# Batch 0's queries in two loads, and the first weights, sums and transposes of a one-core attention and feed-forward kernel in another order

## The chip, the cores and the metric

The kernel runs on one core of one Trainium2 chip. The metric is the device time of one execution in microseconds (us); for a version the median of its runs counts. All times below come from the runs, or from one profiled execution and its trace.

## The reference

Eight batches of linear attention with cosine-weighted features, then a feed-forward layer whose two last products have no nonlinearity between them.

```python
# q, k, v: (8, 8, 576, 64) FP32; w1, w2: (512, 1024); w3: (1024, 1024); w_out: (1024, 512)
theta = np.pi / 2.0 * pos / S                                     # S = 576
phi(x) = concat([relu(x) * cos(theta), relu(x) * sin(theta)], -1) # 64 -> 128 features
kv  = einsum('bhsf,bhsd->bhfd', phi(k), v);   z = phi(k).sum(2)
num = einsum('bhsf,bhfd->bhsd', phi(q), kv)
den = einsum('bhsf,bhf->bhs', phi(q), z)[..., None] + 1e-06
x = (num / den).transpose(0, 2, 1, 3).reshape(8 * 576, 512)       # 4608 tokens
out = ((x @ w1) * (x @ w2)) @ w3 @ w_out
```

## The kernel before, in words

Matmul operands are BF16, sums FP32. The work is written as a list (PLAN) that is walked line by line; each word issues the instructions of one small step on whichever engines it needs, and every engine executes its own instructions in the order in which they were issued. So the list is the schedule, and nothing reorders it.

A batch has 576 positions, held as five chunks: 0 to 3 of 128 rows, 4 of 64. `k b c` and `q b c` make the features of a chunk: the cosine half on DVE (L504), the sine half on ACT (L508) or, for some heads, on DVE (L511). `qt` transposes a chunk of query features on PE (L576) into the PSUM tile pst and copies it to qpT (L580, on ACT or DVE). `kv b` (for batch 0 `kv0`, `ks0`) sums keys times values over the chunks on PE and `kvs0` or the end of `kv` copies the result (kvs). `n b c` is the numerator and denominator of a chunk (L594), `d b c` its division on DVE (L605 to L607, tile xblk), `xt b c` the transpose of the divided rows on PE (L636) with a copy into xT (L637). From batch 1 on most transposes are DMA transposes on SP (`qd`, `xd`).

The feed-forward part goes over nine tiles t of 512 tokens. Each `f t` is one step of it: products of xT with w1 and w2 (L683), the copy of the first (ACT) and its product with the second (DVE, tile abT), then abT times w34b (L766 for tile 0). w34b is w3 times w_out, made once: `t3` transposes a 128-row block of w3 on DVE (L473), `w jp` multiplies it with w_out on PE (L483), and ACT copies the result (L486). Tile 0's products stand ahead of that work, tile 0's output behind it, and batch 1's attention between.

Loads are issued by POOL (GpSimd) from FP32 in memory to BF16, in this order: keys and values of batch 0 (L384), eight blocks of w1 and w2 (`w12`, L980, 256 columns each), then w_out (`wo`, L421) and w3 (`w3`, L415) in quarters by partitions, the last chunk of batch 0's queries (`q04`), then batch 1. A load of POOL goes out only when the eighth load before it has landed. Batch 0's queries, chunks 0 to 3, come on SP's queue at the very start, FP32 to FP32, into q0f. Later loads stand behind a gate: a one-element copy by POOL from a tile that must be written first (`lg` behind asb, `lt` behind a transpose, `lx` behind a division). `idle n` issues n matmuls on zeros that nobody reads (L466).

Of the kernel before, what the change touches and what calls it, by code (L numbers as in the profile page):

```python
# [10 lines left out]
FP32 = mybir.dt.float32  # L11
BF16 = mybir.dt.bfloat16
# [4 lines left out]
P = 128  # L17
H, S, D = 8, 576, 64
# [5 lines left out]
WHOLE = (0, 7)  # L24
MORE = 8
PLAN = """\
q 0 1; idle 1; idle 1; q 0 0 4; idle 1; idle 1; qt 0 1 V; k 0 4; k 0 1 0; qs 0 3; k 0 0 0; k 0 2; idle 1; k 0 3; qt 0 0 A; ks0 4; idle 3; qc 0 3; ks0 1; kv0 4 0; q 0 2; kv0 1 0; ks0 0; kv0 2 0; kv0 4 1; ks0 3; kv0 0 0; ks0 2; kv0 0 1; kv0 3 0; kvs0 0 A; kv0 1 1; kv0 2 1; kv0 3 1; kvs0 1 V; qt 0 2 A; n0 0; n0 1; qt 0 3 N; w12 0 0 2; w12 1 0 2; w12 0 2 2; n 0 1; idle 2; w12 1 2 2; w12 0 4 2; d 0 0; w12 1 4 2; w12 0 6 2; w12 1 6 2; wo 0 0 4; d 0 1; qy 0 3 0 A; xt 0 0 A; wo 1 0 4; wo 2 0 4; wo 3 0 4; w3 0 0 2; w3 1 0 2; w3 2 0 2; w3 3 0 2; w3 0 2 2; w3 1 2 2; w3 2 2 2; w3 3 2 2; wo 0 4 4; wo 1 4 4; ns 0 2; idle 2; qy 0 3 1 V; d 0 2; wo 2 4 4; wo 3 4 4; w3 0 4 2; w3 1 4 2; w3 2 4 2; w3 3 4 2; q04; w3 0 6 2; w3 1 6 2; open; w3 2 6 2; w3 3 6 2; l 1 q 0; l 1 q 1; l 1 k 0
f 0; xt 0 1 A; n 0 3; l 1 k 1
f 0; d 0 3; l 1 v 0
f 0; xt 0 2 A  # L30
f 0
f 0; xt 0 3 V; l 1 v 1
f 0
f 0
f 0
f 0
f 0; clear 1
f 0
f 0
f 0; t3 0  # L40
f 0; lg 2 q 0; t3 1; l 2 k 0; l 2 k 1; l 2 q 1; l 2 v 0
f 0
f 0; t3 2 0 4; t3 3 0 4; t3 2 4 4; t3 3 4 4
w 0 0 4
# [17 lines left out]
f 0  # L62
f 0; qt 1 0 A; v 1 2 V; v 1 3 V
f 0
f 0; kv 1; qt 1 1 A
f 0; n 1 4; d 1 4; k 2 4; k 2 2 2
f 0
# [1 line left out]
f 0; n 1 0; d 1 0; xt 1 4 A; q 2 0 0; q 2 1; lt 3 v 0; xt 0 4 A  # L69
f 0  # L70
f 0; v 2 0 G
f 0
f 0; xt 1 0 V; n 1 1
f 0
f 0
f 1
f 1; lg 3 q 1; d 1 1; qd 2 0; n 1 2; v 2 3 A; k 2 3; d 1 2; qt 1 3 V
# [31 lines left out]
f 2; xd 3 0; n 3 1  # L109
f 2; d 3 1  # L110
f 2; xd 3 1
f 2; q 4 0; q 4 4; n 3 4
f 2; d 3 4; xd 3 4; lg 5 v 0; l 5 v 1
f 2
f 2; q 4 3; v 4 4 V
f 2; q 4 1 0
f 2; k 4 1; k 4 0; qd 4 0; n 3 2
f 2
f 2
f 2; q 4 2  # L120
f 2; lg 5 k 0; l 5 k 1
f 2
f 2; qd 4 3; d 3 2; n 3 3
f 3; k 4 4; k 4 2
# [198 lines left out]
def kernel(  # L323
# [11 lines left out]
    nc = tc.nc  # L335
    B = q.shape[0]
    DM, DFF = moe_w1.shape
# [4 lines left out]
    const = ctx.enter_context(tc.tile_pool(name="const", bufs=1))  # L342
# [19 lines left out]
    osbs += [q0f[:, ts(i, H // 2)].rearrange("p h c d -> p (h c d)").rearrange("p (i m) -> p i m", m=DM) for i in range(2)]  # L362

    def osb_of(i):

# [13 lines left out]
    raw = {}  # L379

    def load_rows(eng, t, rows, half):

        j, span = (5, slice(0, 320)) if half == 0 else (4, slice(320, S))
        eng.dma_start(out=t[ts(half, 64), :, 0:j, :].rearrange("p h j d -> p h (j d)"),  # L384
                      in_=rows[:, span, :].rearrange("h (p j) d -> p h (j d)", j=j))

    def load(b, name, part=None):
        src = {"k": k, "v": v, "q": q}[name]
        if part != 1:
            raw[b, name] = kbufs[b % 2] if name == "k" else ld.tile([P, H, NCH, D], BF16, name=name + "s", bufs=NRQ if name == "q" else NRV)  # L390
        t = raw[b, name]
        if b == 7:
            if part != 1:
                nc.gpsimd.dma_start(out=t[:, :, 0:4, :].rearrange("p h j d -> p h (j d)"),
                                    in_=src[b, :, 0:512, :].rearrange("h (p j) d -> p h (j d)", j=4))
# [29 lines left out]
    def gate(behind):  # L425

        nc.gpsimd.tensor_copy(out=seen[0:behind.shape[0]], in_=behind)  # L427

    def load_q04():
# [33 lines left out]
    def idle_mms(n):  # L463

        for _ in range(n):
            nc.tensor.matmul(unread[:, :], lhsT=zeros[:, 0:128], rhs=zeros[:], start=True, stop=True)  # L466

    idle_mms(16)
    def w3_tr(jp, l0=0, n=8):

        if l0 == 0:
            w3Ts[jp] = sm.tile([P, 8, 128], BF16, name="w3T", bufs=NT3)
        nc.vector.transpose(out=w3Ts[jp][:, l0:l0 + n, :].rearrange("p l (c i) -> p l c i", c=4),  # L473
                            in_=w3b[:, jp, :].rearrange("p (c l j) -> p l c j", c=4, l=8)[:, l0:l0 + n])
# [19 lines left out]
    def att_of(b):  # L494
        if b not in att:
            att[b] = {"kp": kp_bufs[b % NKP], "qp": qp_bufs[b % NQP], "va": va_bufs[b % NVA],
                      "qpT": qpT_bufs[b % 2], "x": {}, "n": {}}
        return att[b]

    def features(dst, rows, c, at, n=H, cos=True, sin=True):  # L500

        R = ROWS[c]
        if cos:
            nc.vector.tensor_scalar(out=dst[:R, c, :, 0:D], in0=rows[:R], scalar1=0.0,  # L504
                                    scalar2=cosv[:R, at:at + 1], op0=ALU.max, op1=ALU.mult)
        if sin:
            if n > 0:
                nc.scalar.activation(out=dst[:R, c, 0:n, D:F], in_=rows[:R, 0:n], func=ACTF.Relu,  # L508
                                     scale=sinv[:R, at:at + 1], bias=0.0)
            if n < H:  # L510
                nc.vector.tensor_scalar(out=dst[:R, c, n:H, D:F], in0=rows[:R, n:H], scalar1=0.0,  # L511
                                        scalar2=sinv[:R, at:at + 1], op0=ALU.max, op1=ALU.mult)

    def prep_k(b, c, n=H, **kw):
        features(att_of(b)["kp"], raw[b, "k"][:, :, c, :], c, NCH + c if b == 7 else c, n, **kw)

    def prep_q(b, c, n=H, **kw):
        rows = raw[b, "q"][:, :, c, :] if b > 0 else q0f[:, :, c, :] if c < 4 else q04[:]
        features(att_of(b)["qp"], rows, c, NCH + c if b in WHOLE else c, n, **kw)

    def prep_v(b, c, copy=None):
# [440 lines left out]
    N = None  # L962
    V, A, G = nc.vector.tensor_copy, nc.scalar.copy, nc.gpsimd.tensor_copy
# [43 lines left out]
    def store_behind_transposes():  # L1007
# [4 lines left out]
    ffn = [ffn_groups(t) for t in range(NT)]  # L1012
    do = {
        "f": lambda t: next(ffn[t]), "w": w34_mm, "w3": load_w3, "wo": load_wout, "w12": w12,
        "l": load, "lg": gated, "lt": behind_transposes, "lx": behind_division, "q04": load_q04, "gx": behind_first_x,
        "k": prep_k, "q": prep_q, "v": prep_v,
        "qc": lambda b, c: prep_q(b, c, sin=False), "qs": lambda b, c, n=H: prep_q(b, c, n, cos=False),
        "kc": lambda b, c: prep_k(b, c, sin=False), "ks": lambda b, c: prep_k(b, c, cos=False),
        "qt": q_tr, "qy": q_copy, "ns": lambda b, c: num(b, c, pfirst), "qh": q_tr_halves, "qd": q_dma, "kv": kv, "kv0": lambda c, *half: kv_first(c, False, *half), "ks0": lambda c: kv_first(c, True), "kvs0": kvs_first,
# [40 lines left out]
```

## Time and profile before

| | us |
|---|---|
| median of 3 runs | 243.5 (242.95 to 244.08) |
| the profiled execution | 243.63 |
| its span | 241.9 |
| PE busy | 234.9 |
| DVE busy | 194.6 |
| ACT busy | 112.9 |
| POOL busy | 81.3 |

The span runs from the first to the last instruction of the profile; the execution's time has 1.73 us around it. Busy times are per engine and overlap. Rows of the timeline give start, length, engine, line, instruction, the tiles it writes and reads, and, in brackets, how long the engine had idled and what ended that. The chain of waits follows the last instruction back to what released it, step by step.

### The profile page before, as it was taken

Reading aid. Unit: us, or ns where it says so; the run is one execution under the profiler, and the core shown is the slowest. Engines: PE = TensorE matmul, PEld = TensorE weight load, DVE = VectorE, ACT = ScalarE, POOL = GpSimd, SP = SyncE. Lnnn points to the kernel's source line nnn. Section 1 sums busy time; section 2 is a strip of 40 time slices with the busy share of each in tenths; the row PEclk is TensorE's granted clock in tenths of the full one; section 3 lists DMA queues with packets and bytes.
Section 4 is the critical chain, followed back from the end, with each engine's and each line's share of the span. In section 5 each row is a group of like instructions: output and inputs, shape, how many; then the busy total and the mean of one; then the engine's idle time right before and its main releaser. Section 6 shows DMA issues by size and latency. Waiting matters only on the chain.

```text
span 241.9 us, 5817 instructions
## 1 busy us (share of the span) xinstructions
PE 234.9 (97%) x2236; PEld 163.6 (68%) x2236; DVE 194.6 (80%) x470; ACT 112.9 (47%) x200; POOL 81.3 (34%) x151
## 2 busy tenths in 40 slices
PE   8899999999999999999999999999999999999993
PEld 2579544566964595688679848875995698484462
DVE  6874585978988947999899998999999788776461
ACT  2754314587755832826465435637164302312321
POOL 8763888541804222700430312021020040272020
PEclk9999999999999999999999999999999999999999
DMA  6999999999999999999999959888456938599934
GB/s 196 192 197 199 164 195 186 198 199 194 178 166 147 128 152 198 181 173 180 132 179 177 114 96 184 149 131 90 76 191 129 130 70 160 115 308 311 259 97 173
DMA packets 84939, 40.48 MB, mean 167 GB/s; under 512 B 48048, under 2 KB 82096, under 8 KB 84912
## 3 DMA queue, kind: packets, MB, share of 16 engines
q0 software_dynamic: 37616, 23.60, 66.2%
q1 hardware_dynamic: 47296, 16.52, 40.4%
q8 instruction: 17, 0.28, 0.4%
q14 instruction: 10, 0.08, 0.1%
HBM read 38.80 MB, written 9.44 MB: 199 GB/s over the span
## 4 chain that ended last, share of the span: by engine, by line
PE 77%; DMA 14%; POOL 5%; DVE 1%; issue 1%; ACT 1%; ACTq 0%; POOLq 0%
PE ffnps L683 46%; PE ffnps L874 13%; DMA kf<-in_k_dram 7%; PE ffnps L766 6%; DMA w2b<-in_moe_w_dram 5%; PE pnum L594 4%; PE pnum L558 4%; DMA early<-in_moe_w_out_dram 2%; POOL early L415 2%; PE ffnmore L874 1%; PE ffnps L807 1%; PE ffnps L783 1%; POOL w2b L980 1%; POOL kf L384 1%; POOL w1b L980 1%
## 5 line engine op out<-in xcount | busy, mean ns | idle before, releaser
L683 PE MATMUL ffnps<-xT,w1b 128*128 128x256 bf16 (+2 forms) x448 | 76.2, 303 | 0.2 <-PE unread L466 0.2
L683 PE MATMUL ffnps<-xT,w2b 128*128 128x256 bf16 (+2 forms) x448 | 76.2, 303 | 0.0
L683 PEld LDWEIGHTS <-w1b 128*128 128x128 bf16 x448 | 41.1, 98 | 19.4 <-issue 1.0
L683 PEld LDWEIGHTS <-w2b 128*128 128x128 bf16 x448 | 40.8, 98 | 19.7 <-issue 0.2
L743 ACT CAST asb<-ffnps 128x512 bf16<-128x512 f32 x40 | 23.4, 585 | 43.0 <-PE ffnps L683 38.4
L749 DVE TENSOR_TENSOR abT<-asb,ffnps 128x512 bf16<-128x512 bf16 x40 | 27.2, 682 | 13.8 <-PE ffnps L683 13.5
L726 ACT CAST asb<-ffnps 128x512 bf16<-128x512 f32 x24 | 14.0, 584 | 34.2 <-PE ffnps L683 27.0
L607 DVE TENSOR_TENSOR xblk<-pnum,den 128x512 bf16<-128x512 f32 (+1 forms) x38 | 26.3, 691 | 1.5
L427 POOL COPY seen<-asb 128x1 bf16<-128x1 bf16 x17 | 3.4, 201 | 60.2 <-ACT asb L726 49.7
L508 ACT ACTIVATE kp<-kf,sinv 128x512 bf16<-128x512 bf16 (+4 forms) x33 | 21.0, 663 | 2.1 <-DMA kf<-in_k_dram 2.0
L508 ACT ACTIVATE qp<-qs,sinv 128x512 bf16<-128x512 bf16 (+6 forms) x30 | 18.3, 628 | 5.0 <-DMA qpT<-qp 2.6
L874 PEld LDWEIGHTS <-abT 128*128 128x128 bf16 x192 | 18.5, 98 | 3.2
L733 DVE TENSOR_TENSOR abT<-asb,ffnps 128x512 bf16<-128x512 bf16 x24 | 16.2, 681 | 5.1 <-PE ffnps L683 5.1
L594 PEld LDWEIGHTS <-qpT 128*128 128x128 bf16 x320 | 15.0, 98 | 4.7 <-DVE xblk L607 0.4
L766 PE MATMUL ffnps<-w34b,abT 128*128 128x512 bf16 x72 | 17.5, 379 | 0.0
L594 PE MATMUL pnum<-kvs,qpT 128*128 128x65 bf16 x304 | 15.7, 194 | 0.1
L874 PEld LDWEIGHTS <-s 128*128 128x128 bf16 x144 | 13.9, 98 | 2.5 <-DVE s L854 0.8
L504 DVE TENSOR_SCALAR kp<-kf,cosv 128x512 bf16<-128x512 bf16 (+1 forms) x40 | 14.1, 372 | 0.6 <-DMA kf<-in_k_dram 0.6
L483 PE MATMUL ffnps<-early,w3T 128*128 128x512 bf16 x64 | 14.3, 379 | 0.0
L384 POOL DMA_DIRECT2D vs<-in_v_dram x16 | 12.0, 757 | 3.6 <-PE ffnps L483 1.3
L504 DVE TENSOR_SCALAR qp<-qs,cosv 128x512 bf16<-128x512 bf16 (+1 forms) x35 | 12.6, 369 | 0.1
L874 PE MATMUL ffnps<-w34b,abT 128*128 128x256 bf16 x96 | 12.4, 273 | 0.0
(145 smaller groups left out, 337.1 us busy)
## 6 DMA issues: line engine op xcount, KB each, us to landing
out_dram<-osb SPq DMA_DIRECT2D x9, 256.0 KB, 3.4
kf<-in_k_dram POOLq DMA_DIRECT2D x7, 320.0 KB, 7.1
early<-in_moe_w_dram POOLq DMA_DIRECT2D x16, 128.0 KB, 5.5
qs<-in_q_dram POOLq DMA_DIRECT2D x6, 320.0 KB, 6.3
vs<-in_v_dram POOLq DMA_DIRECT2D x6, 320.0 KB, 7.3
kf<-in_k_dram POOLq DMA_DIRECT2D x7, 256.0 KB, 8.4
qs<-in_q_dram POOLq DMA_DIRECT2D x6, 256.0 KB, 6.5
vs<-in_v_dram POOLq DMA_DIRECT2D x6, 256.0 KB, 8.3
```

Of the source, the lines that this page charges most:

```text
L384: eng.dma_start(out=t[ts(half, 64), :, 0:j, :].rearrange("p h j d -> p h (j d)"), in_=rows[:, span, :].rearrange("h (p j) d -> p h (j d)", ...
L483: nc.tensor.matmul(acc[:, :], lhsT=w3T[:, lc, :], rhs=woutb[:, lc, :], start=(lc == 0), stop=(lc == 7))
L504: nc.vector.tensor_scalar(out=dst[:R, c, :, 0:D], in0=rows[:R], scalar1=0.0, scalar2=cosv[:R, at:at + 1], op0=ALU.max, op1=ALU.mult)
L508: nc.scalar.activation(out=dst[:R, c, 0:n, D:F], in_=rows[:R, 0:n], func=ACTF.Relu, scale=sinv[:R, at:at + 1], bias=0.0)
L594: nc.tensor.matmul(nt[:, h // 4, ds((h % 4) * 65, 65)], lhsT=qpT[:, h, ds(at, 128)], rhs=kvs[:, h, :], start=True, stop=True)
L607: nc.vector.tensor_tensor(out=xblk[rows, g0:g0 + ng], in0=n4[:, :, :, 0:D], in1=den[rows, 0:ng].unsqueeze(3).to_broadcast([R, ng, 4, D]), ...
L683: nc.tensor.matmul(out, lhsT=w[:, kc, ts(jc, 128)], rhs=x[:, kc, tok], start=(kc == 0), stop=(kc == 3))
L733: nc.vector.tensor_mul(out=abT[:, ts(pair, 2), ts(half, 256)], in0=asb[:].rearrange("p (i n) -> p i n", i=2), in1=bT[:, :].rearrange("p (i ...
L743: nc.scalar.copy(out=asb[:], in_=aT[:, :])
L749: nc.vector.tensor_mul(out=abT[:, jc, :], in0=asb[:], in1=bT[:, :])
L766: nc.tensor.matmul(ops[:, :], lhsT=abT[:, jc, ts(ms, 128)], rhs=w34b[:, jc, :], start=(jc == 0), stop=(jc == 7))
L874: nc.tensor.matmul(into[:, ts(ms, 256)], lhsT=a[:, kc, ts(ms, 128)], rhs=b[:, kc, :], start=(ms == 0 and kc == 0), stop=(ms == 1 and kc == 3))
```

## The change

- q0f is split. Chunks 0 and 1 stay FP32 on SP's queue (q0a). Chunks 2 and 3 become BF16 (q0b), loaded by POOL behind batch 0's values and ahead of w1.
- The start of the plan is rewritten for that: features, transposes, numerators and divisions of chunks 2 and 3 come later, among the first steps of tile 0's products; six idle matmuls fewer at the very start, others placed elsewhere. Clearing va and qp (three small memsets) goes from the start to a place among tile 0's products.
- The first two row blocks of w3 are loaded ahead of the first half of w_out. `t3 0` and `t3 1` stand two steps earlier in the plan.
- Batch 1's `kv` stands two steps of tile 0's output later (each step is two matmuls), and the transpose of batch 1's chunk 0 of x stands one step nearer behind its division.
- Later: batch 4's first two query features stand three steps later; batch 5's keys are loaded four steps sooner, behind a new gate (`lk`, a key feature), and its values behind a division instead of behind asb.

```diff
-    q0f = const.tile([P, H, 4, D], FP32, name="q0f")
+    q0f = const.tile([P, 4 * DM], FP32, name="q0f")
+    q0a = q0f[:, 0:2 * DM].rearrange("p (h c d) -> p h c d", c=2, d=D)
+    q0b = q0f[:, 2 * DM:3 * DM].bitcast(BF16).rearrange("p (h c d) -> p h c d", c=2, d=D)
...
-    nc.sync.dma_start(out=q0f[:].rearrange("p h j d -> p h (j d)"),
-                      in_=q[0, :, 0:512, :].rearrange("h (p j) d -> p h (j d)", j=4))
+    q0_rows = q[0, :, 0:512, :].rearrange("h (p j) d -> p h j d", j=4)
+    nc.sync.dma_start(out=q0a.rearrange("p h j d -> p h (j d)"),
+                      in_=q0_rows[:, :, 0:2, :].rearrange("p h j d -> p h (j d)"))
     s_i = _angles(nc, const)
     load(0, "k")
     load_v0()
     identb = const.tile([P, P], BF16, name="identb")
     make_identity(nc, identb[:])
+    nc.gpsimd.dma_start(out=q0b.rearrange("p h j d -> p h (j d)"),
+                        in_=q0_rows[:, :, 2:4, :].rearrange("p h j d -> p h (j d)"))
...
-    clear_rows(0)
...
-    idle_mms(16)
+    idle_mms(10)
...
+            made[0] = dst[:R, c, 0, 0:1]
...
+    def behind_feature(b, name, part):
+
+        gate(made[0])
+        load(b, name, part)
```

Of the plan, the end of its long first line and the lines around batch 1's sums:

```diff
-... n0 0; n0 1; qt 0 3 N; w12 0 0 2; ...; d 0 1; qy 0 3 0 A; xt 0 0 A; ... wo 0 0 4 ... w3 0 0 2; w3 1 0 2; w3 2 0 2; w3 3 0 2; ...
+... n0 0; n0 1; w12 0 0 2; ...; qs 0 2; qs 0 3; qc 0 2; ...; d 0 1; qc 0 3; idle 3; xt 0 0 A; qt 0 2 A; w3 0 0 2; w3 1 0 2; w3 2 0 2; w3 3 0 2; wo 0 0 4; ...
...
 f 0
+f 0
+f 0
 f 0; kv 1; qt 1 1 A
```

More of the change, by code (lines that the diff above doesn't have):

```diff
@@ L35 @@
 f 0
-f 0
[L37 to L41, printed above, removed]
+f 0; clear 1
+f 0; clear 0
+f 0; t3 0
+f 0; t3 1
+f 0
+f 0; lg 2 q 0; l 2 k 0; l 2 k 1; l 2 q 1; l 2 v 0
 f 0
@@ L71 @@
 f 0; v 2 0 G
-f 0
 f 0; xt 1 0 V; n 1 1
-f 0
 f 0
@@ L111 @@
 f 2; xd 3 1
-f 2; q 4 0; q 4 4; n 3 4
-f 2; d 3 4; xd 3 4; lg 5 v 0; l 5 v 1
+f 2; n 3 4
+f 2; d 3 4; xd 3 4; lx 5 v 0; l 5 v 1
 f 2
-f 2; q 4 3; v 4 4 V
+f 2; q 4 0; q 4 4; q 4 3; v 4 4 V
 f 2; q 4 1 0
-f 2; k 4 1; k 4 0; qd 4 0; n 3 2
+f 2; k 4 1; k 4 0; lk 5 k 0; l 5 k 1; qd 4 0; n 3 2
 f 2
@@ L120 @@
 f 2; q 4 2
-f 2; lg 5 k 0; l 5 k 1
+f 2
 f 2
@@ L360 @@
     osbs += [const.tile([P, 2, DM], FP32, name=f"osb{i}") for i in range(MORE - 2)]
-    q0f = const.tile([P, H, 4, D], FP32, name="q0f")
-    osbs += [q0f[:, ts(i, H // 2)].rearrange("p h c d -> p (h c d)").rearrange("p (i m) -> p i m", m=DM) for i in range(2)]
+    q0f = const.tile([P, 4 * DM], FP32, name="q0f")
+    q0a = q0f[:, 0:2 * DM].rearrange("p (h c d) -> p h c d", c=2, d=D)
+    q0b = q0f[:, 2 * DM:3 * DM].bitcast(BF16).rearrange("p (h c d) -> p h c d", c=2, d=D)
+    osbs += [q0f[:, ts(i, 2 * DM)].rearrange("p (i m) -> p i m", m=DM) for i in range(2)]
     def osb_of(i):
@@ L498, in att_of @@
         return att[b]
+    made = [None]
     def features(dst, rows, c, at, n=H, cos=True, sin=True):
@@ L517, in prep_q @@
     def prep_q(b, c, n=H, **kw):
-        rows = raw[b, "q"][:, :, c, :] if b > 0 else q0f[:, :, c, :] if c < 4 else q04[:]
+        rows = raw[b, "q"][:, :, c, :] if b > 0 else q0a[:, :, c, :] if c < 2 else q0b[:, :, c - 2, :] if c < 4 else q04[:]
         features(att_of(b)["qp"], rows, c, NCH + c if b in WHOLE else c, n, **kw)
@@ L1014 @@
         "f": lambda t: next(ffn[t]), "w": w34_mm, "w3": load_w3, "wo": load_wout, "w12": w12,
-        "l": load, "lg": gated, "lt": behind_transposes, "lx": behind_division, "q04": load_q04, "gx": behind_first_x,
+        "l": load, "lg": gated, "lt": behind_transposes, "lx": behind_division, "lk": behind_feature, "q04": load_q04, "gx": behind_first_x,
         "k": prep_k, "q": prep_q, "v": prep_v,
```

8 lines of the change are left out of this document (4 added, 4 removed).

## The prediction

> **What bounds the kernel now.** I read the page first, then the chain of waits, then the timeline and the transfer rates up to 60 us, where the change acts.
>
> ```profile
> span 241.9 us, 5817 instructions
> PE 234.9 (97%) x2236; PEld 163.6 (68%) x2236; DVE 194.6 (80%) x470; ACT 112.9 (47%) x200; POOL 81.3 (34%) x151
> ```
>
> TensorE (PE) is busy 97% of the span. The profiled execution took 243.63 us, its span and 1.73 around it, and the median of the three runs is 243.5; I add to 243.63. A busy PE only says that there is always something in its pipeline. What releases it is told by the chain of waits, cut to 0 to 60 us and merged:
>
> ```profile
> 13.35 11.00 DMA w2b<-in_moe_w_dram
> 24.35 0.28 issue
> 24.63 2.83 POOL early L415 x5
> 27.47 5.88 DMA early<-in_moe_w_out_dram
> ...
> 38.11 0.65 POOL kf L384
> 38.76 9.06 DMA kf<-in_k_dram
> ...
> 47.90 0.93 ACT kp L508 x2
> ...
> 49.14 0.57 ACT qpT L580
> 49.71 0.04 issue
> 49.75 0.61 PE pst L576 x8
> 50.36 0.86 PE ffnps L766 x4
> 51.22 1.33 PE pnum L558 x40
> ```
>
> The columns are start, length, and what ran. From 13 us to 48 us the chain holds no matmul: it runs over POOL's loads, one behind the other, to the keys of batch 1, and only then over ACT into PE. So the front of the kernel is bound by the stream of loads. The stretches of transfer rate show how full that stream is (last two columns: busy share of the 16 DMA engines, GB/s as written; the first is the stretch and its length, then busy times by engine and the granted clock):
>
> ```profile
> 3.00:4.00 1.00, 1.00 (x4) 0.33 (x3) 0.86 (x6) 0.00 (x0) 1.00 (x3) 1.00 1.09 388
> 13.00:14.00 1.00, 1.00 (x30) 1.00 (x28) 0.22 (x1) 0.38 (x1) 1.00 (x2) 1.00 1.45 197
> 27.00:28.00 1.00, 1.00 (x7) 0.44 (x5) 0.64 (x1) 0.01 (x1) 1.00 (x2) 1.00 1.05 108
> 28.00:29.00 1.00, 1.00 (x6) 0.45 (x5) 0.41 (x3) 0.58 (x1) 0.87 (x3) 1.00 0.83 107
> ```
>
> At 3 us the stream writes 388 GB/s: batch 0's queries arrive as FP32 and are stored as FP32. At 13 us it writes 197, with FP32 turned into BF16, so it reads about 394. The pace is set by the bytes read, near 390 GB/s both times. Only at 27 to 29 us does it fall short, by some 180 KB or 0.9 us.
>
> PE meets that stream here (start, length, engine, line, instruction, and in brackets the idle time before and what ended it):
>
> ```profile
> 38.09 1.30 DVE L473 STREAM_TRANSPOSE w3T<-early 128x512 bf16<-128x512 bf16 x2 [2.46 <-DMA early<-in_moe_w_dram]
> 39.31 0.30 DVE L504 TENSOR_SCALAR qp<-q,cosv 64x512 bf16<-64x512 bf16 x1
> 39.54 0.34 DVE L511 TENSOR_SCALAR qp<-q,sinv 64x512 bf16<-64x512 bf16 x1
> 39.80 1.23 DVE L473 STREAM_TRANSPOSE w3T<-early 128x1024 bf16<-128x1024 bf16 x1
> 40.04 0.61 PE L576 MATMUL pst<-identb,qp 128*128 128x128 bf16 x8
> 40.97 0.38 DVE L580 COPY qpT<-pst 128x512 bf16<-128x512 bf16 x1
> 41.40 0.43 PE L594 MATMUL pnum<-kvs,qpT 128*128 128x65 bf16 x8
> ```
>
> DVE idles 2.46 us until the third pair of w3 blocks lands at 38.09. From there it runs without a pause: that transpose, q04's features, the next transpose, the copy of qpT, which ends at 41.35; PE's num(0,4) starts at 41.40, on its heels. Everything of PE before 41.40 that came earlier would wait here. The chain of waits shows the second such place, at 47.90, where ACT starts batch 1's keys as they land.
>
> **The change part by part.** *Batch 0's queries in two loads.* Chunks 0 and 1 (0.52 MB) stay first on SP; chunks 2 and 3 (0.52 MB) go, as BF16, to POOL behind the values. What the start of the feed-forward waits for today:
>
> ```profile
> 12.27 0.28 PE L952 MATMUL pnum<-vs,kp 128*128 128x64 bf16 x4 [0.22 <-DMA vs<-in_v_dram]
> ...
> 15.86 0.55 POOL L421 DMA_DIRECT2D early<-in_moe_w_out_dram  x1 [0.77 <-DMA w2b<-in_moe_w_dram]
> ...
> 17.02 0.38 PE L683 MATMUL ffnps<-xT,w1b 128*128 128x128 bf16 x4 [0.15 <-PE unread L466]
> ...
> 17.24 0.39 PE L683 MATMUL ffnps<-xT,w2b 128*128 128x128 bf16 x4
> ```
>
> With 0.52 MB less ahead of them, keys and values land 0.52/0.388 = 1.35 us sooner, so attention could feed the first products at 17.02 - 1.35 = 15.7. The first w2 block does not gain: as many bytes are read ahead of it. It has landed at 15.86 (POOL's load eight places behind it goes out then). So the first w2b product moves from 17.24 to about 16.1: PE gains a lead of 1.0 us. The new order of num, transposes and divisions of chunks 2 and 3 may eat 0.5 of that; the lead stays positive.
>
> *Where the lead goes.* The bytes read ahead of the third w3 pair are the same, so 38.09 stands, and with it 41.40. The lead becomes a wait of PE in front of the fifth block of w3·w_out. Worth at the end: 0. That is the step on which the forecast turns.
>
> *What the stream pays.* The segments of these queries fall from 1024 to 512 bytes read (two rows of 64 FP32 in place of four), so 2048 of them in place of 1024, 64 more for each of 16 engines. The nearest rows with small segments are batch 7's last chunk of keys (512 segments of 256 bytes read), which passes at 149 to 151 us:
>
> ```profile
> kf<-in_k_dram POOLq DMA_DIRECT2D x1, 64.0 KB, 5.3
> 149.00:149.50 0.50, 0.50 (x7) 0.44 (x6) 0.39 (x2) 0.39 (x2) 0.00 (x0) 1.00 1.71 186
> 149.50:150.00 0.50, 0.50 (x12) 0.46 (x10) 0.50 (x3) 0.00 (x0) 0.00 (x0) 1.00 1.96 164
> 150.00:150.50 0.50, 0.50 (x12) 0.45 (x9) 0.50 (x2) 0.00 (x0) 0.00 (x0) 1.00 1.88 172
> 150.50:151.00 0.50, 0.50 (x7) 0.45 (x5) 0.50 (x2) 0.00 (x0) 0.00 (x0) 1.00 1.55 178
> 151.00:152.00 1.00, 1.00 (x11) 0.89 (x10) 1.00 (x5) 0.50 (x1) 0.00 (x0) 1.00 1.45 196
> ```
>
> Against 196 the four halves lose (10 + 32 + 24 + 18) x 0.5 = 42 KB, 0.21 us, over 32 segments per engine: 6.7 ns each. 64 more segments cost 64 x 6.7 = 0.4 us. The low end is 0 (bytes alone count), the high end is a 512-byte segment as dear as one of 1024, 1.35 us for each half, 2.7 in all. I take 0.4, by these rows. All that lands behind these queries lands that much later, at 38.09 and at 47.90, and PE with it.
>
> [...]
>
> *POOL's queue.* Behind the last loads of values, before (k, v and w loads are named by the tile they fill):
>
> ```order
> L384 DMA vs<-in_v_dram 64x4x320
> L384 DMA vs<-in_v_dram 64x4x256
> masks.py:197 MEMSET identb 128x128
> masks.py:199 AFFINE_SELECT identb<-identb 128x128
> L980 DMA w1b<-in_moe_w_dram 128x4x256
> ```
>
> and after:
>
> ```order
> L386 DMA vs<-in_v_dram 64x4x320
> L386 DMA vs<-in_v_dram 64x4x256
> masks.py:197 MEMSET identb 128x128
> masks.py:199 AFFINE_SELECT identb<-identb 128x128
> L444 DMA q0f<-in_q_dram 128x8x128
> L987 DMA w1b<-in_moe_w_dram 128x4x256
> ```
>
> One more issue stands ahead of w1b. Its length is that of the load with as many segments (first row below, 0.89 us); it is hidden, since POOL waits for the keys of batch 0 just behind it (second row), and costs at most those 0.9 us if it were not.
>
> ```profile
> L394 POOL DMA_DIRECT2D kf<-in_k_dram x1: 887/887/887, 142.6 to 142.6; - x1
> 8.84 0.74 POOL L980 DMA_DIRECT2D w1b<-in_moe_w_dram  x1 [1.06 <-DMA kf<-in_k_dram]
> ```
>
> Further down the same queue, where w3 (L415, later L417) and w_out (L421, later L423) follow the last block of w2, before:
>
> ```order
> L980 DMA w2b<-in_moe_w_dram 128x4x256
> L421 DMA early<-in_moe_w_out_dram 32x4x512 x4
> L415 DMA early<-in_moe_w_dram 32x8x256 x8
> L421 DMA early<-in_moe_w_out_dram 32x4x512 x4
> L415 DMA early<-in_moe_w_dram 32x8x256 x4
> L431 DMA q_100<-in_q_dram 64x8x64
> ```
>
> and after:
>
> ```order
> L987 DMA w2b<-in_moe_w_dram 128x4x256
> L417 DMA early<-in_moe_w_dram 32x8x256 x4
> L423 DMA early<-in_moe_w_out_dram 32x4x512 x4
> L417 DMA early<-in_moe_w_dram 32x8x256 x4
> L423 DMA early<-in_moe_w_out_dram 32x4x512 x4
> L417 DMA early<-in_moe_w_dram 32x8x256 x4
> L433 DMA q_100<-in_q_dram 64x8x64
> ```
>
> The first w3 pair passes the first half of w_out. The third pair, which PE meets, has the same loads ahead of it as before: 0.
>
> *Batch 1's sums four matmuls later, its first x two sooner.* ACT's queue from the first copies of batch 1's transposed queries (qpT) to the copy of its kv sums (kvs), with tile 0's finished output (early) between, before, then after:
>
> ```order
> L580 COPY qpT_97<-pst 128x8x64
> L580 COPY qpT_97<-pst 128x8x128
> L772 COPY early<-ffnps 128x512
> L580 COPY qpT_97<-pst 128x8x128
> L562 CAST kvs<-pnum 128x260
> ```
>
> ```order
> L587 COPY qpT_97<-pst 128x8x64
> L587 COPY qpT_97<-pst 128x8x128
> L779 COPY early<-ffnps 128x512
> L587 COPY qpT_97<-pst 128x8x128
> L779 COPY early<-ffnps 128x512
> L569 CAST kvs<-pnum 128x260
> ```
>
> A second block of tile 0's output is finished ahead of the sums: four matmuls, 0.86 us by the chain's row, come out from behind them, and x(1,0) has six matmuls instead of eight to hide its division. What it waits for today:
>
> ```profile
> 55.62 0.35 DVE L504 TENSOR_SCALAR kp<-kf,cosv 128x512 bf16<-128x512 bf16 x1 [0.33 <-DMA kf<-in_k_dram]
> 57.42 0.39 PE L636 MATMUL pst<-identb,xblk 128*128 128x128 bf16 x4
> ```
>
> The division of x(1,0) stands on DVE behind batch 2's first keys, which cost it 0.33; with the sums 0.86 later they will have landed. The lost cover is 0.43, the lost wait 0.33, and the copies of the sums keep their own cover. So this lies between -0.3 (the wait goes, the cover was to spare) and +0.4 (the cover was all needed, the wait stays); I take -0.2, nearer to the first, because the keys are loads and the sums now stand later against them.
>
> *The rest at nothing.* Six fewer idle matmuls at the start, and five put together later, touch the lead alone. Clearing va and qp moves to DVE's stretch before the w3 transposes, hidden by the lead. Batch 4's first features and batch 5's loads move among matmuls that follow each other in the chain without a break, 6.26 and 3.45 us long; without that cover it would be one feature, 0.3 us.
>
> ```profile
> 108.93 6.26 PE ffnps L683 x52
> ...
> 118.71 3.45 PE ffnps L683 x16
> ```
>
> Sum: 243.63 + 0.4 - 0.2 = 243.8.
>
> **The rivals.** *Small segments at full price* (the other side, slower): if a 512-byte segment takes an engine as long as one of 1024, or the 256-byte writes of the second half take twice their time, the stream loses 1.35 to 2.7 us ahead of 38.09 and 47.90: 244.8 to 246.1. It decides from 0.8 us of loss on. For it speaks the busy share of 1.96 at 150 us; against it, that the rate fell by a sixth there, at half the segment size. [...]
>
> *Written bytes set the pace* (faster): the second half is written as BF16, 0.26 MB less. At 197 GB/s all loads behind it land 1.33 us sooner, the lead is kept, and the time is 243.63 - 1.33 - 0.2 = 242.1. The 388 GB/s at 3 us speaks against it.
>
> *The hole of 27 to 29 us goes*: POOL's queue has another mix behind w2b's last block; if the stream stays full, 0.9 us come back: 243.8 - 0.9 = 242.9. As many loads of the same sizes stand behind that block as before, so I expect the hole again.
>
> **How the numbers follow.** The forecast has 0.55, its own range 243.4 to 244.6; small segments 0.2; written bytes 0.12; the hole 0.1; 0.03 for the rest. About 0.5% (1.2 us) is what a measurement can tell from no change here. Faster by more: written bytes, and a little of the hole and the rest, 0.17. Slower by more: small segments and the upper edge of the forecast, 0.25. Between: 0.58. The range runs from 242.1, the written bytes, to 245.0, which leaves out most of the small segments' case.
>
> **What would show it.** Right: first w2b products near 16.1 to 16.5, w3's third pair landing at 38.1 to 38.8, a wait of PE of some 0.5 to 1 us before it, batch 1's keys at 47.9 to 48.5. Wrong: that pair landing before 37.5 (then the lead survives), or after 39 (small segments), or a break of over 0.5 us in PE's chain after 60 us.

## The result, and the profile after

The changed kernel takes 246.45 us (median of 11 executions, 244.22 to 247.29), the kernel before 243.83 in the same session; the ratio is 1.0086 [1.0057, 1.0115]. It is slower, by more than the forecast's range allowed. The eleven times lie in two groups, five from 244.2 to 245.2 and six from 246.4 to 247.3. The profiled execution, 246.45 us, is of the upper group. (Some kernels had a few slow executions, over 1.5% above their fastest; medians, counts and ratios leave them out, and a ratio compares all the others, so it need not be the quotient of the medians, here 1.0107.)

From the page of the changed kernel:

```profile
span 244.6 us, 5811 instructions
PE 236.1 (97%) x2235; PEld 164.1 (67%) x2235; DVE 194.6 (80%) x470; ACT 112.5 (46%) x199; POOL 82.2 (34%) x152
```

The span is 2.7 us longer. PE does the same work but for one matmul on zeros, so the question is where it starts late, waits or runs slower: its busy time is 1.2 us longer. The chain of waits of the changed kernel (start, length, what ran; first the front, then 133 to 145 us):

```profile
4.22 7.54 DMA vs<-in_v_dram
11.81 0.28 PE pnum L959 x4
...
14.10 0.44 PE pnum L601 x8
14.54 2.13 PE unread L470 x5
16.67 0.44 PE pst L643 x4
17.14 0.59 ACT xT L644
17.77 0.61 PE ffnps L690 x8
...
23.68 10.44 PE ffnps L690 x80
34.12 7.77 PE ffnps L487 x36
...
133.77 0.34 PE ffnps L690 x4
134.10 10.46 DMA qpT<-qp
144.56 0.05 issue
144.61 0.43 PE pnum L601 x8
```

Before, this chain held loads and their issues alone from 13 to 48 us. Now it holds, but for short pieces of DVE and ACT, PE's own work from 11.8 us on: the front is bound by PE, not by the stream. And five matmuls on zeros ("unread") take 2.13 us in it. The stretches say why (columns: stretch and length, PE busy and its matmuls, granted clock, DMA share, GB/s). Before:

```profile
10.00:12.00 2.00, 1.69 (x38) 1.00 1.41 195
12.00:14.00 2.00, 1.78 (x54) 1.00 1.45 197
14.00:16.00 2.00, 1.91 (x34) 1.00 1.45 196
```

and after:

```profile
10.00:12.00 2.00, 1.20 (x33) 1.00 1.61 185
12.00:14.00 2.00, 1.76 (x54) 0.90 1.53 193
14.00:16.00 2.00, 2.00 (x14) 0.50 1.47 203
```

PE is busy only 1.20 of 2 us at 10 to 12, and then the granted clock falls to a half, from 13.6 to 17.0 us. (The mean over 13.5 to 14.0 is 0.61 and over 17.0 to 17.5 it is 0.97.) The five matmuls on zeros take 2.32 us in it; in a later run, one_load, whose clock stays at 1.00, the same five take 1.24. First the changed kernel, with its first product, then one_load:

```profile
14.35 2.32 PE L470 MATMUL unread<-zeros 128*128 128x512 bf16 x5
17.77 0.38 PE L690 MATMUL ffnps<-xT,w1b 128*128 128x128 bf16 x4 [0.20 <-ACT xT L644]
```

```profile
14.24 1.24 PE L467 MATMUL unread<-zeros 128*128 128x512 bf16 x5
```

The first product waits for x (xT), which stands behind these matmuls. The weights are late too, but had landed by then. POOL sees the first blocks of w1 and w2 land at 15.55 and 16.86, where it saw them at 14.52 and 15.86 before:

```profile
15.55 0.60 POOL L417 DMA_DIRECT2D early<-in_moe_w_dram  x1 [0.64 <-DMA w1b<-in_moe_w_dram]
16.86 0.58 POOL L417 DMA_DIRECT2D early<-in_moe_w_dram  x1 [0.70 <-DMA w2b<-in_moe_w_dram]
```

So the first products move from 17.02 to 17.77, and the first w3·w_out product from 32.27 to 33.96 (before, then after):

```profile
32.27 7.93 PE L483 MATMUL ffnps<-early,w3T 128*128 128x512 bf16 x36
```

```profile
33.96 7.93 PE L487 MATMUL ffnps<-early,w3T 128*128 128x512 bf16 x36
```

DVE no longer waits for w3's third pair but for PE, and late in the kernel stands a wait that was not there:

```profile
38.48 1.31 DVE L477 STREAM_TRANSPOSE w3T<-early 128x512 bf16<-128x512 bf16 x2 [1.08 <-PE ffnps L487]
144.61 0.43 PE L601 MATMUL pnum<-kvs,qpT 128*128 128x65 bf16 x8 [1.43 <-DMA qpT<-qp]
```

The sum, from the timelines: +0.75 at the first product, another 0.94 up to the w3·w_out products (1.69), of which 0.39 is taken up by tile 1's first product (60.06 against 58.76: 1.30); 1.23 is left at 133.5, and 1.43 comes at 144.6: 2.7. One profile of each is a small sample: three other profiles whose front has the loads, the order and the clock of before (kv1_late, late_only and weights, below) start their first product at 16.40 to 16.76, so the profile of before is a late one.

### The profile page after: what moved, and what is told of

It reads as the page before. It is cut to its first block, busy times and chain, and to the rows that moved or that the text cites. A ratio compares the mean times of both kernels' runs of the same rounds, so it can differ in the third digit from the quotient of the medians.

```text
span 244.6 us, 5811 instructions
## 1 busy us (share of the span) xinstructions
PE 236.1 (97%) x2235; PEld 164.1 (67%) x2235; DVE 194.6 (80%) x470; ACT 112.5 (46%) x199; POOL 82.2 (34%) x152
## 4 chain that ended last, share of the span: by engine, by line
PE 79%; DVE 8%; DMA 7%; issue 2%; POOL 1%; ACT 0%; DVEq 0%; POOLq 0%
PE ffnps L690 44%; PE ffnps L881 11%; PE ffnps L487 6%; PE ffnps L773 5%; DMA qpT<-qp 4%; PE pnum L601 4%; PE pnum L565 3%; DMA vs<-in_v_dram 3%; PE ffnmore L881 1%; PE pst L583 1%; DVE abT L756 1%; DVE xblk L614 1%; DVE qp L510 1%; PE ffnps L814 1%; PE unread L470 1%
## 5 line engine op out<-in xcount | busy, mean ns | idle before, releaser
L614 DVE TENSOR_TENSOR xblk<-pnum,den 128x512 bf16<-128x512 f32 (+1 forms) x39 | 26.9, 691 | 1.5
L429 POOL COPY seen<-asb 128x1 bf16<-128x1 bf16 x15 | 2.9, 194 | 51.7 <-ACT asb L733 45.3
L740 DVE TENSOR_TENSOR abT<-asb,ffnps 128x512 bf16<-128x512 bf16 x24 | 16.2, 681 | 5.1 <-PE ffnps L690 5.1
L601 PEld LDWEIGHTS <-qpT 128*128 128x128 bf16 x320 | 15.1, 99 | 7.0 <-DMA qpT<-qp 2.3
L601 PE MATMUL pnum<-kvs,qpT 128*128 128x65 bf16 x312 | 16.4, 196 | 1.6 <-DMA qpT<-qp 1.4
L773 PE MATMUL ffnps<-w34b,abT 128*128 128x512 bf16 x72 | 17.5, 380 | 0.0
L386 POOL DMA_DIRECT2D vs<-in_v_dram x16 | 12.7, 805 | 2.6 <-PE ffnps L487 1.2
L510 DVE TENSOR_SCALAR qp<-qs,cosv 128x512 bf16<-128x512 bf16 (+1 forms) x35 | 12.1, 357 | 0.1
```

The lines of the kernel that those rows point to most:

```text
L601: nc.tensor.matmul(nt[:, h // 4, ds((h % 4) * 65, 65)], lhsT=qpT[:, h, ds(at, 128)], rhs=kvs[:, h, :], start=True, stop=True)
L614: nc.vector.tensor_tensor(out=xblk[rows, g0:g0 + ng], in0=n4[:, :, :, 0:D], in1=den[rows, 0:ng].unsqueeze(3).to_broadcast([R, ng, 4, D]), ...
L740: nc.vector.tensor_mul(out=abT[:, ts(pair, 2), ts(half, 256)], in0=asb[:].rearrange("p (i n) -> p i n", i=2), in1=bT[:, :].rearrange("p (i ...
L773: nc.tensor.matmul(ops[:, :], lhsT=abT[:, jc, ts(ms, 128)], rhs=w34b[:, jc, :], start=(jc == 0), stop=(jc == 7))
```

## The experiments

Each ran in a session with the kernel before, whose executions spread too: 123 of them over six sessions have a mean granted clock of 0.996 or more in 112 (median 243.41) and less in 11 (median 244.16). Half the clock for 3.4 of some 242 us makes a mean of 0.993, so this number tells whether an execution without a trace had a dip of the length of the one above, though not where. Of the changed kernel's eleven executions nine dip, the five of the lower group among them; two of the upper group do not (246.79 and 247.24). So the dip is not what parts the two groups.

**Parts of the plan alone.** The late lines (batch 4's features, batch 5's loads and gates) put back in the changed kernel:

```diff
-f 2; d 3 4; xd 3 4; lx 5 v 0; l 5 v 1
+f 2; d 3 4; xd 3 4; lg 5 v 0; l 5 v 1
...
```

> The changed kernel with its plan around batch 4's features and batch 5's loads put back as before. Theory (two losses: the front, about 1.2 us, in every execution; and a wait of 1.4 us for batch 4's transposed queries in about half of them, made by the later loads of batch 5): 244.8 to 245.2, no run above 246.0, and no wait of PE for qpT at 144 us. Rival (one loss: the later front shifts the loads against the transposes, and the wait comes with that): as the changed kernel, some runs above 246.4, median about 246.

Measured: 245.32, ratio 1.0067 [1.0043, 1.009]; no time above 245.8, no wait at 144 us, span still 1.9 over before. Three of the six executions dip. Then these lines alone, on the kernel before:

> The kernel before with only the plan lines around batch 4's features and batch 5's loads of the changed one. Theory of two losses: runs near 243.8 and runs near 245.2, median between 244.2 and 245.2. Rival (the front does it all): 243.8, no run above 244.8.

Measured: 243.05, 0.9985 [0.9965, 1.0006]. Alone they cost nothing. With the front of the changed kernel six of eleven executions lie above 246.4, and without these lines none of six; but the intervals of the two ratios overlap, and early_w below, which has these lines as before and no dip, has two of six above 246.8. Batch 1's sums two steps later, alone:

```diff
+f 0
+f 0
 f 0; kv 1; qt 1 1 A
...
-f 0
 f 0; xt 1 0 V; n 1 1
-f 0
```

> The kernel before with batch 1's sums two steps later and its first x transposed two steps nearer behind its division, nothing else. The prediction gave this -0.2 us (between -0.3 and +0.4): 243.2 (243.1 to 243.8). Rival: the cover of x(1,0)'s division was all needed, or the copies of the sums stand open, +0.3 to +0.5, and PE shows a wait of that length between 52 and 60 us.

Measured: 243.74, 1.001 [0.9993, 1.0027]: not told from nothing, so neither the -0.2 nor a cost of 0.4 is shown. The first w3 blocks ahead of w_out, alone:

```diff
-wo 0 0 4; ... wo 3 0 4; w3 0 0 2; ... w3 3 0 2;
+w3 0 0 2; ... w3 3 0 2; wo 0 0 4; ... wo 3 0 4;
```

> The kernel before with the first two w3 row blocks loaded ahead of the first half of w_out, nothing else. The prediction gave this 0, since the third w3 pair has the same bytes ahead of it: 243.2 to 243.6, that pair landing at 38.1. Rival: another mix behind the last w2 block fills the hole of 27 to 29 us (107 GB/s), the pair lands up to 0.9 us sooner and the time falls by as much, 242.5. Rival: w_out's later landing holds up the first w3-w_out product, 244 or more.

Measured: 243.59, 1.001 [0.9993, 1.0026]. The hole of 27 to 29 us was half filled (198 and 148 GB/s) and DVE's wait for the third pair was gone, without any gain.

**The load.** late_back, with batch 0's queries in one FP32 load as before:

```diff
-    nc.sync.dma_start(out=q0a..., in_=q0_rows[:, :, 0:2, :]...)
-    nc.gpsimd.dma_start(out=q0b..., in_=q0_rows[:, :, 2:4, :]...)
+    nc.sync.dma_start(out=q0w..., in_=q0_rows...)
```

> The changed kernel with the late lines of the kernel before (as in late_back, 245.3 us, 1.9 over before) and, besides, batch 0's queries in one FP32 load on SP as before: the new order of the front with the old load. Theory (two parts of one size): the second load in front of w1 and w2 makes their blocks land 1 us later, and the work of chunks 2 and 3, now behind the first product, costs another 1 us; here only the second part is left: the first w2 block seen near 15.9, the w3-w_out products starting 0.8 to 1.2 us after the 32.3 of before, 244.3 to 244.7 us. Rival, all from the load and its segments: as before, 243.4 to 243.8. Rival, all from the order of PE's work: as late_back, 245.1 to 245.5.

Measured: 244.09, 1.0038 [1.0017, 1.0059], 1.2 less than late_back by the medians, though the two intervals overlap. The timeline of PE:

```profile
16.44 0.38 PE L687 MATMUL ffnps<-xT,w1b 128*128 128x128 bf16 x4
16.66 0.39 PE L687 MATMUL ffnps<-xT,w2b 128*128 128x128 bf16 x4
```

The products start 0.58 sooner than before, the w3·w_out products 0.37 later (32.64): the work of chunks 2 and 3, now behind the first product, costs 0.95 there. That price hardly depends on the load: from the first product to the first w3·w_out product it is 15.25 us in all seven profiles with the order of before, and 16.2 in eleven of the thirteen with the new order. In the other two, clock_kept and early_w, PE waits for loads on the way. The same with the late lines as changed, so that nothing but the load is undone:

> The changed kernel with nothing undone but the load: batch 0's queries in one FP32 load on SP; the late lines stay as changed. Theory: the 1.4 us wait for batch 4's transposed queries at 144 us comes from the late lines meeting a front that is 1.2 us late; here the front is 0.4 to 0.6 late, so most runs are without it: median 243.9 to 244.5. Rival, the late lines cost 1 us or more on any front but that of before: median 245 or more, in two groups, with that wait in the profile.

Measured: 243.91, 1.0027 [1.0011, 1.0043], none of eleven executions with a dip. So the two loads carry some 2 of the 2.6 us by the medians (1.4 of 2.1 by the ratios), and all the rest of the change about 0.5.

**What it is in the load: the clock or the weights.** late_back with eight more matmuls on zeros between batch 0's sums:

```diff
-ks0 1; kv0 4 0; kv0 1 0; ks0 0; kv0 2 0; kv0 4 1; ... kvs0 1 V; n0 0;
+ks0 1; idle 2; kv0 4 0; idle 2; kv0 1 0; ks0 0; kv0 2 0; idle 2; kv0 4 1; ... kvs0 1 V; idle 2; n0 0;
```

> As late_back, with eight more matmuls on zeros in PE's gaps between 10 and 14 us. Theory (half the granted clock from 13.8 to 17 us is most of the front's loss): granted clock 1.00 throughout, first w2b product at 16.9 in place of 17.99, 243.9 to 244.4, that is 0.7 to 1.1 below late_back. Rival (the moved work of chunks 2 and 3 among the products, or the stream, is what counts): clock restored, but the time within 0.3 of late_back.

Measured: 245.17, 1.0064 [1.004, 1.0088], none of six with a dip. The clock was kept and nothing won, though in late_back itself the executions without a dip have a median of 244.70 and those with one 245.53. In the profile PE now waits for the other limit:

```profile
17.63 0.40 PE L690 MATMUL ffnps<-xT,w2b 128*128 128x128 bf16 x4 [1.12 <-DMA w2b<-in_moe_w_dram]
```

So the second load went behind the first two weight blocks (a plan word behind `w12 1 0 2`):

> late_back with the load of chunks 2 and 3 (BF16, POOL) moved behind the first block of w1 and the first block of w2. Theory: the weights' landing is half of the loss: the first w2 block is seen 1 us earlier, near 15.7, the first w2b product starts near 16.5 to 16.9 and not at 17.5, and the time is 244.3 to 244.7. Rival, the order of PE's work behind the first product (or the features of chunks 2 and 3, which now come later still): 245.2 or more. Rival, small segments alone: they stay, 245.2.

Measured: 246.98, 1.0136 [1.0104, 1.0168]; missed, and three of four executions dip. The first w2 block is seen at 14.51, but ACT and PE meet the features and transposes of chunk 2 ahead of the first product, and these now wait for the load, which ACT sees at 15.68 (first product 17.53, behind xT). With those moved behind the first products as well, and eight matmuls on zeros to keep the clock:

> late_back (245.3 us) with the load of chunks 2 and 3 behind the first blocks of w1 and w2, with their features, transposes and sums behind the first products, so that no wait for that load stands ahead of these, and with seven more matmuls on zeros (as in clock_kept) between batch 0's sums. Theory: the start needs both the weights early and the clock; with both, the clock stays at 1.00, the first w2b product starts at 16.0 to 16.6, the w3-w_out products at 32.0 to 32.8 (the work of chunks 2 and 3 still lies behind the first product), and the time is 243.8 to 244.3, as in one_load. Rival, the small segments or the written BF16 slow the whole stream: 245 or more, with batch 1's keys later than 48.5.

Measured: 245.97, 1.0107 [1.0081, 1.0133], without a dip; missed again. The first product starts at 15.60 with the clock at 1.00, but the second half lands at 16.5, and PE waits for chunks 2 and 3 (timeline of PE):

```profile
17.27 0.62 PE L587 MATMUL pst<-identb,qp 128*128 128x128 bf16 x8 [0.40 <-ACT qp L519]
...
21.34 0.42 PE L605 MATMUL pnum<-kvs,qpT 128*128 128x65 bf16 x8 [0.59 <-DVE xblk L618]
```

The w3·w_out products start at 33.74, nearly as late as in the changed kernel (33.96). With the second half on POOL's queue, it is late or the weights are. Over the profiles this is clear of their spread: with the loads of before the first w2 block is seen at 15.1 to 16.0 (seven profiles), with the second half ahead of it on POOL at 16.3 to 17.9 (six).

**Segments, place or type.** late_back with both halves as FP32, back to back on SP, then late_back with the second half on POOL as FP32:

> late_back (245.3 us) with both halves of batch 0's queries as FP32, back to back on SP at the start; the segments stay at 512 bytes. With one load the same kernel took 244.1. Theory (the queue place: behind the values and ahead of the weights, the second half takes the stream's bytes when the first products need theirs, and 4 to 10 us run below the full rate): 243.9 to 244.4, the first w2 block seen near 15.4 to 15.9, batch 0's values as late as before, no dip of the clock. Rival (512-byte segments cost the stream): 244.8 to 245.3, the first w2 block seen 0.6 us or more later than with one load.

> late_back with the second half where the change put it (POOL, behind the values) but written as FP32. Theory of the place: 245.0 to 245.5 as late_back, the written type makes no difference, a dip of the clock in about half of the runs. Rival, the BF16 writes of 256 bytes are what slows 10 to 14 us (182 to 193 GB/s at a busy share of 1.6): 244.4 or less, the first w2 block seen near 16.2.

Measured: 244.91 (1.0088 [1.0054, 1.0121]) and 245.60 (1.0078 [1.0049, 1.0107]). The written type is not it: with FP32 the first w2 block is seen at 17.14, with BF16 (late_back) at 16.66. And with both halves on SP the weights are early (15.48) and the time is lost all the same: three of seven executions dip (246.3 to 247.3), four do not (244.7 to 244.9). The stretches of two_sp:

```profile
10.00:12.00 2.00, 1.56 (x28) 1.00 1.41 195
12.00:14.00 2.00, 2.00 (x51) 0.62 1.45 196
```

The first half lands at 5.15 us, 1.4 sooner than before; PE does its transposes sooner and then waits 0.86 us for the first key features. Both halves on SP alone, on the kernel before:

> The kernel before with batch 0's queries in two FP32 loads on the same queue, segments of 512 bytes in place of 1024, nothing else. If small segments cost what the prediction took (0.4 us for both): POOL's first issue behind w1b's first block 0.2 to 0.4 us later than 14.52, and the time 243.8 to 244.3. If a segment costs the same whatever its size: w1b 2.7 us later and the time above 245.5. If only bytes count: no change, 243.8.

Measured: 244.34, 1.0035 [1.0016, 1.0054]. Its front is not late (third pair 37.80); the profile waits 0.54 us at 154.6, behind SP's queue. SP's rows of sp_halves, then of before:

```profile
142.10 3.67 SPq L631 DMA_TRANSPOSE xT<-xblk  x2
146.27 1.24 SPq L533 DMA_TRANSPOSE qpT<-qp  x1
```

```profile
142.02 3.67 SPq L629 DMA_TRANSPOSE xT<-xblk  x2
145.79 1.25 SPq L531 DMA_TRANSPOSE qpT<-qp  x1
```

SP pauses 0.50 us between them and not 0.10; two_sp and two_sp_clock, the other kernels with two loads on SP, show 0.52 at the same place, and the seventeen kernels without, 0.10 to 0.11. The pause comes with the second load on SP, 140 us later; why is not shown. So the next try kept both halves on SP and added twelve more matmuls on zeros, to keep the clock:

> two_sp (245.6 us; its four executions with a mean clock of 0.998 or more took 244.7 to 244.9, the three others 246.3 to 247.3) with twelve more matmuls on zeros around batch 0's sums, to keep the clock. Theory (two limits beside each other: the second half on POOL makes the weights late, the earlier first half leaves PE without work at 8 to 11 us and the clock drops): with the weights early (first w2 block seen at 15.5) and the clock at 1.00 all through, the first w2b product starts at 16.2 to 16.8, the w3-w_out products at 32.2 to 32.9, and the time is 244.0 to 244.6, no run above 245.5. Rival (the segments cost the stream or the late transfers whatever the clock): 245.2 or more.

Measured: 245.4, 1.0081 [1.006, 1.0103]; missed. No dip, weights early, but these matmuls stood in the way of the sums (first w2 product 17.30, 0.64 later than with one load), and behind SP's pause PE waited:

```profile
156.50 1.03 PE L690 MATMUL ffnps<-xT,w1b 128*128 128x256 bf16 x8 [1.26 <-ACT asb L733]
```

The pause is avoided with the second half on ACT's queue, here on the kernel before:

```diff
+    for c0, queue in ((0, nc.sync), (2, nc.scalar)):
+        queue.dma_start(out=q0f[:, :, c0:c0 + 2, :]..., in_=q0_rows[:, :, c0:c0 + 2, :]...)
```

> sp_halves (244.3 us; +0.9 over before) with the second half on ACT's queue, so that SP's queue holds as many instructions as before. In the traces with two loads on SP, SP pauses 0.5 us ahead of the four transposes at 146 us (0.1 in all others), and the time is lost there, at 151 to 156 us. Theory (segments cost nothing, SP's pause does): SP's pause is 0.1, no wait near 154, 243.2 to 243.7. Rival (the 512-byte segments cost the stream 0.4 us and more, as the prediction had it): 243.9 to 244.5, w3's third pair later than 38.1.

Measured: 244.3, 1.0045 [1.0025, 1.0065]; neither expectation as it stood. The profiled execution, without a dip, is as fast as before (span 241.6; third pair 37.66, no pause), and the six executions without a dip have a median of 243.72. Six others dip (median 244.93). So 512-byte segments cost nothing that shows in the stream (that pair at 37.66, and at 38.09 before). Those six lie 0.2 to 0.3 above the kernel before, which six values from 243.26 to 244.37 do not tell from nothing. But a dip is more frequent with two loads: in six of twelve executions here, in three of nine of sp_halves, in 11 of 123 of the kernel before. At last late_back with both halves early, the second on ACT's queue, and three more matmuls on zeros where PE had nothing to do (`idle 7` for `idle 4`):

> two_sp (245.6 us) with the second half on ACT's queue and three more matmuls on zeros (seven for four) where PE waited 0.86 us for batch 0's first key features. Theory: weights early, no pause on SP, no dip of the clock or a rare one: first w2b product at 16.4 to 17.0, the w3-w_out products at 32.4 to 33.0, 243.9 to 244.4 as with one load. If the clock dips all the same, the executions with a dip take 245.3 to 246.3. Rival (two loads cost 0.7 us or more whatever the queue and the clock): 244.7 or more without a dip.

Measured: 244.58, 1.0051 [1.003, 1.0071]; one dip in eleven. A little above the expected 243.9 to 244.4; its ten executions without a dip have 244.51, those of one load, ten too, 244.06. Its stretch:

```profile
10.00:12.00 2.00, 1.73 (x34) 1.00 1.40 194
```

**The clock alone.** The kernel before without four matmuls on zeros:

```diff
-k 0 2; idle 1; k 0 3; qt 0 0 A; ks0 4; idle 3; qc 0 3;
+k 0 2; k 0 3; qt 0 0 A; ks0 4; qc 0 3;
```

> The kernel before without the four matmuls on zeros that stand between its transposes and batch 0's sums (8.5 and 10 us), nothing else: the price of the clock alone, with the stream untouched. Theory: the clock falls to 0.5 for 2 to 4 us between 12 and 17 us in most runs, the first products start 0.5 to 1.2 us later, and of that the wait for the third w3 pair absorbs little: 244.2 to 245.0. Rival (the lead of PE is worth nothing at the end, as the prediction had it): 243.2 to 243.7 in spite of a dip. No dip: 243.4, and nothing is told.

Measured: 244.41, 1.0033 [1.0014, 1.0053]; ten of eleven executions dip, the other took 243.19. The stretches of dip, and its first w2 product:

```profile
10.00:12.00 2.00, 1.15 (x32) 0.97 1.41 195
12.00:14.00 2.00, 1.95 (x47) 0.50 1.45 196
```

```profile
18.32 0.39 PE L683 MATMUL ffnps<-xT,w2b 128*128 128x128 bf16 x4
```

The product is 1.08 later than before (17.24), with the stream untouched (first w2 block seen at 16.00), and 0.8 to 0.9 of it is there at the end. This is the price of the clock by itself.

**The late wait.** The changed kernel with batch 5's loads and gates back, then with batch 4's features back:

```diff
-f 2; d 3 4; xd 3 4; lx 5 v 0; l 5 v 1
+f 2; d 3 4; xd 3 4; lg 5 v 0; l 5 v 1
...
```

```diff
-f 2; n 3 4
+f 2; q 4 0; q 4 4; n 3 4
...
```

> The changed kernel with batch 5's loads at their old places and behind their old gates; batch 4's features stay three steps later. Theory: the new gates (a division, a key feature) made these loads 4 to 6 us later, and the DMA transposes on SP behind them; with the old gates no wait at 144 us, no run above 246, median 245.0 to 245.4 as late_back. Rival, the later features of batch 4 make its transposes late: the runs fall in two groups as those of the changed kernel (244.2 to 245.2 and 246.4 to 247.3), median 246.

> The changed kernel with batch 4's first two query features back at their old place; batch 5's loads stay at the changed places and gates. Theory: the wait at 144 us stays, runs in two groups, median 245.5 to 246.5. Rival (the later features are its cause): no run above 246, median 245.0 to 245.4.

Measured: 244.93 (1.0077 [1.0047, 1.0107]; two of nine above 247) and 245.91 (1.0102 [1.008, 1.0124]; two of six above 246.4). In the changed kernel the new gates made POOL issue batch 5's values at 102.2 and its keys at 106.2 us, where it was 98.1 and 100.1, although the keys stand four steps sooner in the plan. In feats_back they are as late (103.3 and 106.8). Neither profile has the wait. The medians lie as the theory of the loads had it, but four of the nine executions of loads_back dip and all six of feats_back, and those with a dip are alike (245.1 to 247.3 and 245.1 to 246.8). So these runs favour neither half.

## Why the prediction was wrong, point by point

- **"PE gains a lead of 1.0 us ... The new order ... may eat 0.5 of that; the lead stays positive."** This step failed: the lead of +0.5 to 1 became a lag of 1.69 at the w3·w_out products. Three terms were wrong.
  - The clock, which the prediction did not have at all. In the changed kernel's profile it is what makes the first product late: with the five matmuls on zeros at 1.24 us and not 2.32, x could have been there up to 1.1 us sooner. Taken alone (dip) it costs 0.8 to 0.9.
  - The weights. "As many bytes are read ahead of it" holds, but the first w2 block came 1.0 us later (16.86 against 15.86), not on time. With the clock kept it is the next limit: PE waits 1.12 for it in clock_kept. Part of it is a slower stream: 168 to 177 GB/s written at 4 to 10 us where it was 185 to 203 at 10 to 16, which makes some 0.7 us (estimate: the shortfall against 195). Why it is slower is not shown; that POOL's loads run without SP's is not enough, since early_w, with no other loads either, wrote 193 to 198 from 5 to 10 us. The values, reckoned 1.35 us sooner, were 0.46 sooner than before (11.81 against 12.27) and no more than 0.1 sooner than in one_load, where that product runs at 11.94 without a wait, although the first half of the queries itself came 1.3 us sooner.
  - The new order: 0.95 by one_load, where the prediction had up to 0.5.
- **"Worth at the end: 0. That is the step on which the forecast turns."** The forecast did turn on it, but with the sign reversed. A lead with the stream as it was is in no run. A lag is not worth 0: 1.08 at the first product was worth 0.8 to 0.9 (dip), so the stream's slack behind PE was 0.2 to 0.3 us there, and 0.39 in the changed kernel. In the seventeen profiles without a second load on SP the first w3·w_out product starts anywhere from 31.65 to 35.05 us, and the span is that start and 209.4 to 210.6 us more: what moves that start moves the end.
- **"Six fewer idle matmuls at the start ... touch the lead alone."** Such matmuls can keep the clock: without four of them, at 8.5 to 10 us in the kernel before, ten of eleven executions dip. That it is the six of the very start whose absence brings the dip here is in no run; what shows is that the three of these four that ran at 10.02 before run at 9.15 now, as PE's work comes sooner, and that PE then waits for values, 0.80 us between 10 and 12. PE busy 1.14 to 1.62 of 2 us at 10 to 12 went with a dip in seven profiles, and 1.68 or more with none in twelve; q0b_behind dips at 1.77 (1.46 at 9 to 11), and sp_halves does not with 1.11 at 8 to 10, so the share alone does not decide. No single long gap stood ahead of it: the longest one of PE from 8 to 13.6 us in the changed kernel is 0.39. The dip itself has a granted clock of 0.50 and lasts 3.4 us there, 13.6 to 17.0 us (6.8 in half_pool_f32, 11.6 to 18.4); the stretch ahead of it was sparse, not idle. What decides between a dip and none is not shown.
- **"64 more segments cost 64 x 6.7 = 0.4 us."** Mis-sized: the third pair, to come 0.4 later than 38.09, is there at 37.66 and 37.80 (37.40 to 38.09 in four profiles with the load of before), and of a cost of 0.4 nothing shows. The rival *small segments at full price* gave 244.8 to 246.1 and came near the measured time for another reason.
- **The hole of 27 to 29 us** was predicted to stay; it went (188 to 198 GB/s) and was worth nothing, since the pair no longer bound PE; in weights too it was half filled without any gain.
- **Batch 1's sums, -0.2; the weights' order, 0**: the second stands; the first is within what kv1_late can't tell.
- **The late lines, hidden by "matmuls that follow each other", 0.3 without that cover**: right on the front of before (late_only). On a front that is 1.2 us late, a wait of 1.43 opened at 144.6 in the profiled execution. It is one of the signs of being wrong that the prediction named, "a break of over 0.5 us in PE's chain after 60 us". That it is what sets the upper group of times apart fits the 1.4 to 2 us between the groups, but only that execution has a trace, and early_w has such times without these lines.

Not settled: which half of the late lines opens that wait, what makes the upper group, and why two_act stays 0.5 above one_load. In their profiles that stands from batch 0's sums on: PE starts them at 10.06, behind key features, and not at 9.61, sees values at 11.73 and not 11.12, and its first product (17.01 against 16.44) and w3·w_out (33.21 against 32.64) are both 0.57 later. No kernel here is measurably faster than before; late_only is the nearest.

## What to carry to other kernels

Here splitting a load in a full stream made its first half early (1.3 us), and, with the second half behind other loads, something else late (the first w2 block, 1.0 us). List what reads each load and when, the filler of an engine included: in the changed kernel work that came early left a hole behind it (PE busy 1.20 of 2 us at 10 to 12, and the clock at 0.50 from 13.6), and while the values came 0.46 us sooner, a dip alone cost 0.8 to 0.9 at the end. Two limits ended within about a us of each other here (x, used at 17.77 us, and the first w2 block, seen at 16.86): clock_kept took away one of them and showed no gain (245.17 against 245.32), which does not acquit it. And where times spread, sort them by the granted clock of each execution before comparing medians.

## What the runs showed of the hardware

- A dip of TensorE's clock comes in some executions of one and the same program and not in others: 11 of 123 of the kernel before, 10 of 11 without four matmuls on zeros, 6 of 12 with the queries in two halves. Between the medians with and without, it costs 0.75 us in the kernel before, 0.6 in sp_halves and 1.2 in act_half, and more in two kernels with only two or three such executions: 1.9 in one_load, 2.1 in two_sp.
- Its length in the profiles is 3.4 us (the changed kernel) or 6.8 (half_pool_f32), at a granted clock of 0.50, and the longest gap of PE ahead of it was 0.39 us in the changed kernel (8 to 13.6 us).
- In two_sp the clock fell behind the sparse stretch, not in it: it was 1.00 at 10 to 12 us, with PE busy 1.56 of 2 us, and 0.62 at 12 to 14, when PE was busy 2.00 of 2 us with batch 0's sums.
- One more load at the start of SP's queue went with a pause of 0.5 us between two groups of DMA transposes 140 us later (0.1 otherwise, seventeen kernels), and not when that load was on ACT's queue.
